# A hand-written instruction order dealt anew for the first two batches of a fused attention and SwiGLU kernel

## The chip, the cores and the metric

The kernel runs on one core of a Trainium2 chip. The metric is the device time of one execution in microseconds. TensorE (PE in the profile), VectorE (DVE), ScalarE (ACT), GpSimd (POOL) and SyncE (SP) each take their instructions in the order in which the program issued them; transfers are started from the queues of SP and ScalarE (SPq and ACTq).

## What is computed

Eight batches of 512 tokens and 32 state slots, 8 heads of 64. Tokens read the states, the states read the tokens, and the 8 x (512 + 32) rows that come out pass an RMS norm and a SwiGLU layer (512 to 1536 to 512). The reference, cut to what matters:

```python
a = softmax(scale * x @ state.T)          # per batch and head
xread = a @ state                         # 512 token rows
a2 = softmax(scale * state @ x.T)
sread = a2 @ x                            # 32 state rows
r = rows of [xread, sread], heads side by side   # (8*544, 512)
rn = r / sqrt(mean(r*r) + 1e-6) * rms_g
out = (silu(rn @ w_gate) * (rn @ w_val)) @ w_out
```

## The kernel before, in words

Everything stays in SBUF in a feature-major layout, one batch after another. Softmax reads are kept as weights over the state slots (aT_s), so the hidden layer of a batch is the product of aT_s with the batch's own weights: w_gate and w_val times the batch's states (own_weights, product at L695, ScalarE copy at L707). The three weight matrices come in 64-bit words; 18 pieces are converted to 32 bits in the first stretch, the exponent on ScalarE (exponents(), L246, L249, L252) and the mantissa on VectorE (values(), L273, L276, L282). values() also loads the next raw piece (L212) and stores the finished w_m to w_d (L286), both on SP's queue.

Batch 0 runs with plain products of 512 columns (ORDER). Batches 1 to 7 use seven products of half size in place of eight (hidden_seven), and the output layer the same twice over (project_twice), with sums of weights made at the end of ORDER and in batch 1 and fetched back from DRAM (w<-t_d, L1091). FIRST is batch 1, PERIOD batches 2 to 6, LAST batch 7, STATES the 256 state rows.

**What sets the order.** No scheduler: each part of the work is a Python generator that yields after a step, and a string of letters says which generator goes on next. One letter issues all the instructions of a step, on whatever engines it has, and its transfers. Each engine works off its own instructions in that order and waits (by semaphore) for data and for a free buffer or PSUM bank. So a letter's place in the string is its place in every queue that it uses. A number behind a letter counts that letter from the start of its string: h17 is the 17th h.

Letters of ORDER (400 steps):

| letters | work |
|---|---|
| a, b | batch 0's token read, first and second 256 tokens. a1 transposes the states' rows (L463); a4, a7, b1, b4 transpose x (L499), a5, a8 and the like copy it, a6, a9 are scores (L504); a10 maximum, a11 and b8 subtraction (L512), a12 and b9 exponential; a13 to a15 gram matrix and scaled states; then, a16 on and b10 on: sum (L522), reciprocal, scaling (a18, b12, L527), transposes (a19, b13, L532), a ScalarE copy (a20, b14, L535), gram product (a21, b15, L539), VectorE product (a22, b16, L543), sums of squares (a23, b17, L548), a24, b18 (L552), the power on GpSimd (a25, b19, L299), a26, b20 spread along rows (L306), the last scaling (a27, b21, L558) |
| s, S | batch 0's and batch 1's states read: s1 scores (L568), s2, s3 copies (L574), s4, s5 maxima (L588), s6 (L591), s7, s8 exponentials (L595; S4, S5), s9, s11 transposes (L605), s10, s12 copies (L607), s13 and s14 products over the tokens, s15 scaling (L631 and on) |
| A | batch 1's token read: A1 to A10 transposes of states and x (L317, L328) and copies (L330), A11 scores, copies (L369), A18, A21 exponentials (L411), A31 a product over the states (L437) that takes four PSUM banks |
| e, d | exponents in three steps a piece, values in four, the third of them (d3, d7, ...) without an instruction; piece 0 goes in two halves (e1 to e6, d1 to d8) |
| v | batch 0's own weights, a product and two copies for each of 6 pairs (v1, v4, v7, ...) |
| h, t, u | batch 0's hidden layer, 12 blocks: h(2m+1) gate and h(2m+2) value products (L738), t(m+1) Silu on ScalarE (L744), u(m+1) gated product on VectorE (L748). Two PSUM buffers turn in these products, so a gate product waits for the t of the block before, a value product for its u |
| p, c | output layer of batch 0 (L945), two steps a block, copies and stores (L962) |
| k, Q, w | sums of the output weights on VectorE (L988, then quarters, L1100), slot sums of batch 1 (L760) and its own weights for the first two pairs |
| z | one dummy product of the identity matrix in a bank that nothing reads (L1281); 16 of them |

Letters of FIRST (326 steps):

| letters | work |
|---|---|
| h, t, u | hidden layer in sevens: products of four 256-wide parts (L842); t copies banks to g and c (L889, L892, L894) and applies Silu (L896); u sums and gates on VectorE (L905 to L930) |
| v, x | own weights of batch 1's pairs 2 to 5: product (L695); copies and GpSimd sums (L707, L722) |
| a, s | batch 2's reads: a3 to a6 VectorE transposes (L338), a7 the write to x_d (L340) and a8 to a11 the reads back (L345), both on ScalarE's queue, a12 scores; s: the write to e_d (L616) and four reads back (L620), on ScalarE's queue too (s8 is the first) |
| p, c, k, o | output layer in seven times seven (L1146), copies (L1159), sums, stores (L1257) |
| q, G, g, f, l, w | quarters of the output weights and their fetch (L1091), fetches of w_m from w_d (L195), loads of a later batch, batch 2's first own weights |

The piece of code that reads the strings:

```python
for stream in ORDER:
    if stream in "ckw" and "s" not in seven:
        early.close()
        open_late()
    next(streams[stream])
```

Of the kernel before, what the change touches and what calls it, by code (L numbers as in the profile page):

```python
# [22 lines left out]
FLAT = 1793.0  # L23

ORDER = (
    "zzaaazazbabaeaadbdbaababbzeeeadazbedbabzszezazzbbeadadzbsdaebzzdbeabddzeabdeabAs"
    "zaAeeAadAAbabesavdAabvvAAaAhhssddstdedhueeedAdptddedddpdheuveddvvpdeheeAtedpdAed"
    "dehAedhAheutdAddeApSvdAdApuSvesAdppAvhedAddetdeAsAsehshuAedhtdedpdesdpvevAuvepsd"
    "sdedhdddedseAehApteeduddAAddhAephdveddpetvveudeAAphhAdSAedddthedpduAAAAdeedtdhvA"
    "SupdeSSvevShtAdhAhhdAkSkkkkAutAkSSupAwkkSwkskSpQpQwpQpQkcQQQwScswQpSkcQpwcwwQQQw"  # L30
)

PERIOD = (
# [4 lines left out]
)  # L38

FIRST = (  # L40
    "vahtaqhhaqataaxhthqhuavhquuqhttxhqhutxhhqtuhauuaqhuhaqahtGthqxtxuqhqftuqfhuquxhh"
    "tqtuqvauaGhahhaaaasuthxxtuhhutshxtuauhaafhuthutGvagxhhkaukksxhuhuxthuaatthhutuhh"
    "uhuuutppukuuhpuupkpkpkpfspkpakppkpapcppkkskckpppkakkppapaappckakaapckppkpkpkaspk"
    "pasgkaacckpapakgpgoagpkppksklkapppagpakkakospsopskoppapkklsswwswkpgxxxppopxoxcfc"
    "fxssoo"
)
LAST = (
    "vhhtfthhthxuhguxhtvvhutuhxfhtuthuhhuhhxtuthfxhtuxtxuhxhuhuvtauhhhthxuuthkxthuhhh"
# [1339 lines left out]
```

## Time and profile before

| | us |
|---|---|
| three runs | 744.66, 746.24, 746.92 |
| their median | 746.24 |
| the profiled execution's own time | 744.98 |
| its span in the trace | 743.0 |
| TensorE busy in it | 735.2 (99%) |
| VectorE busy | 578.5 (78%) |
| ScalarE busy | 379.7 (51%) |
| GpSimd busy | 258.9 (35%) |

The span runs from the first to the last recorded instruction, so it lies 2.0 us under the execution's time. Times in rows of a timeline are microseconds from the span's start. A row gives start, duration, engine, source line, operation, what is written and read, and how many instructions it joins; brackets hold the idle time ahead of it and what ended it. Matmuls overlap in the pipeline, so the distance from start to start says more of TensorE's pace than a duration. In the table by stretch, a row has the stretch, its length, the busy time of PE, PEld (loading of weights), DVE, ACT and POOL with the number of instructions, TensorE's granted clock, the busy share of the transfer engines, and GB/s.

### The profile page before, as it was taken

To read this page: it belongs to the slowest core of one execution; us is meant where nothing else is said; L and a number is where in the kernel's file an instruction comes from. 1 tells how busy PE (TensorE), PEld (TensorE's weight loads), DVE (VectorE), ACT (ScalarE), POOL (GpSimd) and SP (SyncE) were. 2 spreads that over 40 slices of the span, in tenths; PEclk is the share of its full clock that TensorE was granted. 3 is DMA by queue.
4 is the path that set the end of the run, shared out by engine and by line. 5 is a ranking of instruction groups with operands and counts; after the bars stand their busy time and mean duration, and the time that the engine had idled before them with its cause. 6 is when DMAs were issued, how large, how long until landed. Compare 5 with 4: busy or idle time off the path is not lost.

```text
span 743.0 us, 14235 instructions
## 1 busy us (share of the span) xinstructions
PE 735.2 (99%) x5582; PEld 590.6 (79%) x5582; DVE 578.5 (78%) x957; ACT 379.7 (51%) x635; POOL 258.9 (35%) x362
## 2 busy tenths in 40 slices
PE   8999999999999999999999999999999999999998
PEld 6634444779977998789878997799778987899996
DVE  3998989899846994699659984799469955798862
ACT  5999982473265725472366426562547336511220
POOL 3100005431373128512563228312841267324400
PEclk9999999999999999999999999999999999999999
DMA  9997936964792278607881669328860883063311
GB/s 294 279 328 239 355 158 228 322 281 134 204 343 61 91 284 278 199 1 297 234 294 28 232 207 319 93 90 299 272 188 4 315 230 130 1 223 117 133 55 28
DMA packets 60994, 146.15 MB, mean 197 GB/s; under 512 B 14848, under 2 KB 31744, under 8 KB 54016
## 3 DMA queue, kind: packets, MB, share of 16 engines
q1 hardware_dynamic: 47808, 125.78, 48.9%
q10 hardware_dynamic: 13120, 19.47, 9.4%
q8 instruction: 44, 0.72, 0.4%
q14 instruction: 22, 0.18, 0.1%
HBM read 116.46 MB, written 28.77 MB: 195 GB/s over the span
## 4 chain that ended last, share of the span: by engine, by line
PE 94%; DMA 3%; DVE 1%; ACTq 0%; issue 0%; ACT 0%; SPq 0%
PE f L842 36%; PE f L1146 31%; PE pv L738 6%; PE f L945 5%; PE pv L695 3%; PE f L1008 2%; DMA x_d<-xB 2%; PE at L695 2%; PE at L631 1%; PE f L1281 1%; PE at L355 1%; PE at L437 1%; DVE w L1100 1%; DVE xB L338 1%; DMA rows<-in_state_dram 1%; PE pv L504 1%
## 5 line engine op out<-in xcount | busy, mean ns | idle before, releaser
L842 PE MATMUL f<-aT_s,v 128*128 128x256 f32 x504 | 119.0, 381 | 0.1
L842 PEld LDWEIGHTS f<-aT_s,v 128*128 128x128 f32 x504 | 94.8, 191 | 19.6 <-DVE h L1200 4.2
L905 DVE TENSOR_TENSOR g<-g,f 128x512 f32<-128x512 f32 x84 | 55.9, 684 | 64.0 <-PE f L842 40.3
L842 PE MATMUL f<-aT_t,vs 128*128 128x256 f32 x336 | 86.7, 382 | 0.5 <-ACT g L889 0.5
L1174 POOL TENSOR_TENSOR kept<-kept 128x256 f32<-128x256 f32 x28 | 20.9, 745 | 182.8 <-DVE kept L1186 116.1
L1159 ACT COPY kept<-f 128x512 f32<-128x512 f32 (+1 forms) x56 | 30.0, 538 | 98.3 <-PE f L1146 97.6
L1146 PE MATMUL f<-w,h 128*128 128x128 f32 x588 | 74.7, 276 | 0.0
L842 PEld LDWEIGHTS f<-aT_t,vs 128*128 128x128 f32 x336 | 62.9, 190 | 13.1 <-issue 5.0
L722 POOL TENSOR_TENSOR vs<-v 128x256 f32<-128x256 f32 x42 | 31.1, 740 | 115.0 <-ACT v L707 114.8
L1146 PEld LDWEIGHTS f<-w,h 128*128 128x128 f32 x588 | 69.8, 192 | 1.2 <-issue 0.8
L896 ACT ACTIVATE hb<-g 128x1024 f32<-128x1024 f32 x42 | 44.5, 1058 | 48.1 <-DVE g L905 44.4
L918 DVE TENSOR_TENSOR hb<-hb,f 128x512 f32<-128x512 f32 (+1 forms) x48 | 31.2, 650 | 27.9 <-PE f L842 27.9
L299 POOL TENSOR_TENSOR ri<-ss,mhalf 128x4 f32<-128x4 f32 (+1 forms) x9 | 9.3, 1029 | 124.3 <-ACT ss L387 102.6
L945 PE MATMUL f<-wo,hb 128*128 128x512 f32 x96 | 44.5, 600 | 0.0
L738 PE MATMUL pv<-aT_s,v 128*128 128x512 f32 x96 | 43.9, 596 | 0.0
L842 PE MATMUL f<-aT_t,v 128*128 128x256 f32 x168 | 43.6, 382 | 0.0
L842 PE MATMUL f<-aT_s,vs 128*128 128x256 f32 x168 | 43.4, 381 | 0.0
L1146 PE MATMUL f<-wo,hb 128*128 128x128 f32 x336 | 42.3, 275 | 0.0
L1146 PE MATMUL f<-wo,h 128*128 128x128 f32 x336 | 42.1, 275 | 0.0
L1146 PEld LDWEIGHTS f<-wo,hb 128*128 128x128 f32 x336 | 40.4, 192 | 0.4
L918 DVE TENSOR_TENSOR hb<-hb,c 128x512 f32<-128x512 f32 (+1 forms) x48 | 35.7, 744 | 6.0 <-ACT hb L896 5.7
L1146 PEld LDWEIGHTS f<-wo,h 128*128 128x128 f32 x336 | 39.8, 192 | 0.0
(227 smaller groups left out, 1637.0 us busy)
## 6 DMA issues: line engine op xcount, KB each, us to landing
w_m<-w_d SPq DMA_DIRECT2D x48, 1024.0 KB
w<-t_d SPq DMA_DIRECT2D x49, 576.0 KB
out_dram<-kept SPq DMA_DIRECT2D x28, 256.0 KB
raw<-in_moe_w_val_dram SPq DMA_DIRECT2D x6, 1024.0 KB
raw<-in_moe_w_out_dram SPq DMA_DIRECT2D x6, 1024.0 KB
w_d<-w_m SPq DMA_DIRECT2D x6, 1024.0 KB
x_b<-in_x_dram SPq DMA_DIRECT2D x6, 1024.0 KB
x_d<-xB ACTq DMA_DIRECT2D x6, 1024.0 KB
```

The costliest lines, as they stand in the source:

```text
L695: TE.matmul(out=pv[e][Ns * j:Ns * j + Ns, :], lhsT=stT_g[b][D * e:D * e + D, j, :], rhs=w[D * e:D * e + D, j].rearrange("p m k f -> p (m k ...
L722: GE.tensor_tensor(out=vs[:, 0], in0=a21, in1=a22, op=ALU.add)
L738: TE.matmul(out=to[0], lhsT=lhs(i, k), rhs=r, start=(i == 0), stop=(i == len(rhs) - 1))
L842: TE.matmul(out=ps[:, i, 0:half], lhsT=l[:, i, :], rhs=r, start=(start and i == 0 and k == 0), stop=(k == len(lhs) - 1), skip_group_check= ...
L896: SE.activation(out=hb[:, 2 * mp:2 * mp + 2, 0:n].rearrange("p m (c t) -> p m c t", c=2), in_=q["g"][:, :, :, 0:half], func=ACTF.Silu if s ...
L905: VE.tensor_tensor(out=to, in0=to, in1=q[ps][:, :, 0:half], op=ALU.add)
L918: VE.tensor_tensor(out=part, in0=part, in1=val, op=ALU.mult)
L945: TE.matmul(out=banks[r], lhsT=hb[:, m, P * r:P * r + P], rhs=wo[:, m, :], start=(m == 0), stop=(m == NM - 1))
L1008: TE.matmul(out=banks[name][:, r, :], lhsT=lhs(k)[:, P * r:P * r + P], rhs=rhs(k), start=(start and r == 0 and k == 0), stop=(k == HM - 1) ...
L1146: TE.matmul(out=to[half][:, slot, :], lhsT=lhs[:, k, :], rhs=rhs[:, k, :], start=(fresh and n in (0, 4) and k == 0), stop=(k == QM - 1), s ...
L1159: SE.copy(of_half(k, i), banks[name][i])
L1174: GE.tensor_tensor(out=k[:, 4:8:3], in0=k[:, 5:6].to_broadcast([P, 2, QD]), in1=k[:, 4:8:3], op=ALU.add)
```

## The change

Only two strings are different: ORDER, which covers batch 0 and the start of batch 1 and 2 (the profile up to 126.9 us), and FIRST, batch 1 (up to 210.4 us). Each holds the same letters as often as before, each generator still runs its own steps in its own order, and PERIOD, LAST and STATES are untouched. So the program has the same instructions, and what differs is how the streams interleave in each queue.

```diff
@@ -23,11 +23,11 @@
 FLAT = 1793.0
 
 ORDER = (
-    "zzaaazazbabaeaadbdbaababbzeeeadazbedbabzszezazzbbeadadzbsdaebzzdbeabddzeabdeabAs"
-    "zaAeeAadAAbabesavdAabvvAAaAhhssddstdedhueeedAdptddedddpdheuveddvvpdeheeAtedpdAed"
-    "dehAedhAheutdAddeApSvdAdApuSvesAdppAvhedAddetdeAsAsehshuAedhtdedpdesdpvevAuvepsd"
-    "sdedhdddedseAehApteeduddAAddhAephdveddpetvveudeAAphhAdSAedddthedpduAAAAdeedtdhvA"
-    "SupdeSSvevShtAdhAhhdAkSkkkkAutAkSSupAwkkSwkskSpQpQwpQpQkcQQQwScswQpSkcQpwcwwQQQw"
+    "zzzaaazazbabaaabdebdbadeabeazszbbeadebeezdzbazzaabbaszeabbazzddbebeaaezbddabddsa"
+    "eAbzAAdaeasAbAaeAvsavvbaAdsdAdsAhdtdAhehudpdpeedthdeededdevupddvevpddAeehdeddteh"
+    "dAAAdeheuAAdeSSedhddpvAtudAdeAAvvpdphhdAshAAteshAueepdetpSedesAeddAdedpsdduddsde"
+    "psvevvdedpAhsddeedddtheeeAedehvsvuvAeAhddpddtpAduedpheAAdAedAehdAhtSddSAdevvdvuA"
+    "phhtAdheSudAheAtAtdphkkuSkAkkkkuAkSSASkwkpSwQsQwpQppwwpskSQpcQkSQScpcQQwQcwwQwQQ"
 )
 
 PERIOD = (
@@ -38,11 +38,11 @@
 )
 
 FIRST = (
-    "vahtaqhhaqataaxhthqhuavhquuqhttxhqhutxhhqtuhauuaqhuhaqahtGthqxtxuqhqftuqfhuquxhh"
-    "tqtuqvauaGhahhaaaasuthxxtuhhutshxtuauhaafhuthutGvagxhhkaukksxhuhuxthuaatthhutuhh"
-    "uhuuutppukuuhpuupkpkpkpfspkpakppkpapcppkkskckpppkakkppapaappckakaapckppkpkpkaspk"
-    "pasgkaacckpapakgpgoagpkppksklkapppagpakkakospsopskoppapkklsswwswkpgxxxppopxoxcfc"
-    "fxssoo"
+    "vaaahahatthhqxthaxuqhahutthtxuhquuqhtahqhaauqahluvtvuhhhtquxqqqhttqxuhqxquhxqufx"
+    "hhtahqtuqahhxuthaautsahahuuhtGahtvuauthkaahuxauhuhxtshhuautgxuahkhtuGthtkhuuuhuu"
+    "khutppushpuupukapkkkppkkcakpppcpkkfpkkGppagkpppppaapsaakpkpckfpapkfkckasokppaaaa"
+    "kpsscskpappapkpgpppgksskagaoppkcagppksaakppkaapwpkpspskskwoxkwxkxppxpfxokglcopsc"
+    "foxsoo"
 )
 LAST = (
     "vhhtfthhthxuhguxhtvvhutuhxfhtuthuhhuhhxtuthfxhtuxtxuhxhuhuvtauhhhthxuuthkxthuhhh"
```

The moves that the prediction speaks of:

- **Up to h1**: the third z stands ahead of a1 (two were there before). d5 goes ahead of b10; d6 and d8 go behind a18 and b16; d10 goes ahead of a22; s5 goes up 11 places, ahead of a26, and d13 down 8.
- **ORDER after h1**: t4 goes behind A15 and e30; p8 and s9 behind h11; s8 behind A21, ahead of t5; v13 ahead of s15; t8 behind e50; t10, which stood ahead of S4 and S5, behind them and e55; the k steps are mixed with u12 and others.
- **FIRST**: v3 ahead of h17; s8 up by 21 places, ahead of c6 and a43; f2 to f4 down by 40 to 120 places, behind G2 and g2; l1 up past stores; steps of h, t, u, q, x by a few places each.

## Prediction

> **What bounds the kernel now.** I read the page first, then a table of busy time by stretch, then the timelines of single engines. From the page: the span, TensorE's row, and the chain that ended last.
>
> ```profile
> span 743.0 us, 14235 instructions
> ...
> PE 735.2 (99%) x5582; PEld 590.6 (79%) x5582; DVE 578.5 (78%) x957; ACT 379.7 (51%) x635; POOL 258.9 (35%) x362
> ...
> PE 94%; DMA 3%; DVE 1%; ACTq 0%; issue 0%; ACT 0%; SPq 0%
> ```
>
> The table by stretch is cut where the kernel changes: up to the first product of the hidden layer (29.5), the rest of ORDER (126.9), then FIRST, with 2 us of it apart. After the length come the engines' busy times.
>
> ```profile
> 0.00:29.50 29.50, 25.90 (x171) 20.07 (x171) 17.95 (x37) 20.61 (x30) 7.75 (x37) 1.00 0.94 281
> 29.50:126.90 97.40, 97.40 (x481) 41.22 (x483) 86.87 (x120) 80.17 (x102) 9.35 (x9) 1.00 0.74 269
> 126.90:143.00 16.10, 16.10 (x110) 11.76 (x110) 13.07 (x23) 7.21 (x13) 6.26 (x9) 1.00 0.92 322
> 143.00:145.00 2.00, 1.53 (x8) 1.06 (x7) 1.48 (x4) 1.97 (x4) 0.00 (x0) 1.00 0.98 179
> 145.00:210.40 65.40, 65.37 (x583) 55.82 (x582) 56.17 (x99) 30.58 (x59) 25.21 (x33) 1.00 0.65 212
> ```
>
> TensorE idles 0.5 us between 29.5 and 210.4, and the change adds and removes no instruction. So a new order can win only in the 29.5 us before h1 and at that one hole; anywhere else it can only open holes. VectorE (86.87 of 97.40) and ScalarE (80.17) are close behind it in ORDER, so holes are easily opened.
>
> **The start.** Before h1 TensorE works beside dummies (z), and VectorE sets the pace. Its rows from the second half's scaling (b12) on, some left out; then the power on GpSimd (a25); then TensorE's transposes b13 and the first product h1:
>
> ```profile
> 18.18 0.69 DVE L527 TENSOR_TENSOR eS<-eS,z 128x512 f32<-128x512 f32 x1
> ...
> 21.23 0.68 DVE L282 SCALAR_TENSOR_TENSOR w_m<-raw,ex 128x512 f32<-128x512 f32 x1
> 21.85 0.69 DVE L543 TENSOR_TENSOR eS<-aT_s,pv 128x512 f32<-128x512 f32 x1
> ...
> 23.18 1.23 DVE L276 SCALAR_TENSOR_TENSOR raw<-top,raw 128x1024 f32<-128x1024 int32 x1
> ...
> 24.72 0.69 DVE L543 TENSOR_TENSOR eS<-aT_s,pv 128x512 f32<-128x512 f32 x1 [0.25 <-PE at L317]
> ...
> 27.92 1.42 DVE L558 TENSOR_TENSOR aT_s<-aT_s,pv 128x512 f32<-128x512 f32 x2
> 29.26 0.68 DVE L588 TENSOR_REDUCE m<-sS 128x1 f32<-128x512 f32 x1
> ```
>
> ```profile
> 26.89 1.15 POOL L299 TENSOR_TENSOR ri<-ss,mhalf 128x2 f32<-128x2 f32 x1 [1.56 <-DVE ss L552]
> ```
>
> ```profile
> 19.33 0.60 PE L532 MATMUL at<-ident,eS 128*128 128x128 f32 x4
> ...
> 29.49 1.96 PE L738 MATMUL pv<-aT_s,v 128*128 128x512 f32 x4
> ```
>
> VectorE's last scalings (a27, in the row at 27.92) end at 29.3, and h1 follows at 29.49. ScalarE's order up to its copy A8 is the same in both strings, so it moves nothing here. On VectorE, d5 goes ahead of b10, which ends b12 (the row at 18.18) 0.4 later, while b13 came behind dummies at 19.33, later than b12's end, and now has one dummy fewer ahead of it: nothing. d6 and d8 go behind a18 and b16, so VectorE reaches b16 at 21.4 instead of 21.85. But b16 needs b15's product, which hangs on ScalarE's unmoved copy and ends about 21.7: 0.4 to 0.5 us of VectorE are lost. d10 (1.23) goes ahead of a22, whose wait of 0.25 it fills. Then s5 (0.68) takes the place of d13 (0.69). Sum up to a27: +0.45 - 0.25 = +0.2. The branch over GpSimd says slightly more: a22 starts 0.35 late, so do a24, the power of 1.15 behind it and a27. I take +0.3; from below it is 0 (b16 not late), from above +0.6 (d6 alone, were nothing filled).
>
> **ORDER after h1.** A step of TensorE (h or p, four 512-wide products) costs 1.72 us: twelve rows from 47.61 to 52.76 are three steps, 5.15.
>
> ```profile
> 47.61 5.31 PE L738 MATMUL pv<-aT_s,v 128*128 128x512 f32 x12
> 52.76 1.88 PE L945 MATMUL f<-wo,hb 128*128 128x512 f32 x4
> ```
>
> Every gate product h(2m+1) waits for the copy t(m-1) that frees its bank, each value product for u(m-1), each output step p for its u. Prices of ScalarE between them (a conversion act and its closing one, and the exponential of the states):
>
> ```profile
> L246 ACT ACTIVATE lin<-raw,bounds 128x1024 f32<-128x1024 int16 x17 | 21.3, 1251 | 0.0
> L252 ACT ACTIVATE ex<-ex,bounds 128x1024 uint16<-128x1024 int16 x17 | 19.5, 1148 | 0.3
> ...
> L595 ACT ACTIVATE e<-sS,s 128x512 f32<-128x512 f32 x4 | 2.9, 727 | 0.0
> ```
>
> A table load (1.28, in a row below) stands before every change between the exponentials (L411, L595) and Silu (L744). The new string has as many changes, five in ORDER and three in FIRST, so loads cancel. I walked TensorE's new order against ScalarE's and VectorE's, adding these prices from p5, where both strings have the same work behind them (52.76 before, 53.1 now):
>
> - p5, v7, p6, p7, h9, h10 bring TensorE to h11 at 62.9. Now p8 and s9 no longer stand ahead of h11. It needs t5. ScalarE, counted from t4 (moved behind A15 and e30, to about 55.3) through a load, A18, e31, v8, v9, A21, s8 and the second load (1.28 + 0.6 + 1.25 + 3 x 0.6 + 0.7 + 1.28 + 0.6, so 7.5, and some 0.15 for A21's wait on VectorE), ends t5 at 62.95: +0.1.
> - v13 is now ahead of s15, which frees its bank. s15 follows d60 on VectorE, 83.75 against TensorE's 83.6: +0.15. Behind v13 on TensorE queue h16 and p13.
> - A31 needs all four banks; the last is freed by u8, which needs t8, now behind e50. It comes at 90.25 against 90.2: +0.05 to 0.1.
> - h21 needs t10. Before, t10 ran ahead of both exponentials of batch 1's states; now S4 and S5 and two loads stand ahead of it:
>
> ```profile
> 98.47 0.59 ACT L744 ACTIVATE t<-pv 128x512 f32<-128x512 f32 x1
> 99.08 1.28 ACT L595 ACT_TABLE_LOAD   x1
> ```
>
> t9 ends at 96.45; load 1.28, S4, S5, e55, two copies and the second load (0.72 + 0.72 + 1.25 + 2 x 0.5 + 1.28) put t10 at 102.7 to 103.3, and TensorE is there at 102.9: +0.4.
>
> The moved k steps run in VectorE's waits, with u12 behind; p21 covers them. Together +0.3 + 0.7 = +1.0 us by the end of ORDER. Each walked margin is good to perhaps 0.3, so these waits lie between 0 and 2.
>
> **FIRST.** The one hole is here. ScalarE issues the reads of x_d (a8 to a11) only once its write (a7) has landed, with t8 and t9 queued behind; h17 waits for t9.
>
> ```profile
> 131.89 0.40 ACTq L340 DMA_DIRECT2D x_d<-xB  x1
> ...
> 140.82 2.17 ACTq L345 DMA_DIRECT2D xG<-x_d  x4
> 143.99 0.57 ACT L889 COPY g<-f 128x512 f32<-128x512 f32 x1
> ```
>
> ```profile
> 142.35 1.03 PE L842 MATMUL f<-aT_t,vs 128*128 128x256 f32 x4
> 143.21 1.03 PE L842 MATMUL f<-aT_t,v 128*128 128x256 f32 x4
> 144.70 1.10 PE L842 MATMUL f<-aT_t,vs 128*128 128x256 f32 x4 [0.47 <-ACT g L889]
> ```
>
> Four products take 0.86 (142.35 to 143.21), so h17 could have started at 144.07: 0.63 lost, of which the page calls 0.47 idle. I take 0.7 with what the next steps wait. The new string sets v3 (0.9) ahead of h17, and TensorE comes 1.0 later, so it reaches h17 at about 145.9, when even a write landing 1 us later has let t9 through: -0.7. Of other moves, s8 goes up 21 places, so that ScalarE waits for e_d with c6 and a43 queued behind. The write left at 190.26 and was answered by 195.76:
>
> ```profile
> 190.26 0.35 ACTq L616 DMA_DIRECT2D e_d<-eB  x1
> ...
> 195.76 0.31 ACTq L620 DMA_DIRECT2D e<-e_d  x1
> ...
> 204.16 1.09 PE L695 MATMUL pv<-w_m,stT_g 64*32 64x512 f32 x16
> ```
>
> c6 then runs about 197; by my walk TensorE's next step into its bank (p40) comes 1.5 later: nothing, or 0.5 if that write lands 2 us later. On SP's queue f2 to f4 fall by 40 to 120 places, behind G2 and g2. g2 waits for a buffer that an outer product of the output frees, but f2 stands ahead of it, and its weights are wanted only at 204.16: nothing. l1, a small load, goes up 221 places on SP past such fetches and costs two issues there.
>
> Sum: +0.3 + 0.7 - 0.7 = **+0.3 us**. The profiled execution took 744.98 us, its span 743.0. So its like would take 745.3. The three runs before lie from 744.66 to 746.92, and 746.24, their median, is 1.26 above the profiled one. On that scale the forecast is 746.24 + 0.3, **746.5 us**: no change.
>
> **Rivals.** *The clock comes up earlier.* TensorE's first rows:
>
> ```profile
> 1.76 2.07 PE L1281 MATMUL f<-ident 128*128 128x256 f32 x4 [1.76 <-POOL ident masks.py:199]
> 5.67 0.45 PE L463 MATMUL at<-ident,rows 128*128 128x128 f32 x1 [1.83 <-DMA rows<-in_state_dram]
> ...
> 6.76 1.06 PE L499 MATMUL at<-ident,x_b 128*128 128x128 f32 x4
> 7.62 1.06 PE L1281 MATMUL f<-ident 128*128 128x256 f32 x2
> ...
> 10.47 0.61 PE L499 MATMUL at<-ident,x_b 128*128 128x128 f32 x4
> 10.92 1.00 PE L504 MATMUL pv<-apart,xT 128*128 128x64 f32 x8
> ```
>
> Four transposes take 0.86 us from 6.76 (to 7.62) and 0.45 from 10.47: TensorE runs at half speed until about 10, though the clock column reads 1.00. Full speed came some 4.2 us after the steady work that begins at 5.67. The work of 1.76 did not count, or the wait for rows undid it. The new string puts z3 into that wait and leaves 1.0 of its 1.83. If a wait so short no longer undoes it, the switch comes 4.2 after 1.76, at 6. The 4.3 us up to 10 then shrink to half, bar what was full already: -1.8 through a8, VectorE and h1, to 744.7. For it: two thirds instead of two fifths of the time from 3.1 to 6.5 are busy. Against: no row shows a switch across any wait. [...]
>
> *ScalarE becomes the bound of ORDER (slower).* Four of the margins above are under 0.2 and hang on ScalarE alone. If it comes one conversion act (1.25) later than walked at t5, h11 starts 1.25 late, and with 0.8 more at t10 the end is +2.0 over the forecast, 748.5. It decides from the point where t5 ends after 63.2. For it: ScalarE is busy 80.17 of 97.40. Against: no step of TensorE waited for it there (97.40 busy of 97.40).
>
> *The order changes nothing that TensorE feels.* Every step covered: +0 - 0.7, 745.5, inside the forecast's range.
>
> **Chances.** Forecast with its neighbours 0.44, clock 0.28, ScalarE 0.24, all covered 0.04. A measurement of this kernel tells about 0.3% (2.2 us) from no change: under 744.0 is faster, over 748.5 slower. From the forecast come 0.34 same, 0.04 faster (none of its waits of 1.0, and a little of the clock) and 0.06 slower (its waits at their upper end of 2, with one more like them). From the clock, half faster, half same, as 744.7 lies 0.7 from the bound and the waits of ORDER decide: 0.14 and 0.14. From ScalarE, with 748.5 as its smallest price, 0.18 slower and 0.06 same. All covered is same. Faster 0.18, same 0.58, slower 0.24. The range for 8 in 10 goes from 743.4 (the clock, without the waits of 0.3 and 1.0 of the forecast) to 749.0 (ScalarE, and the 0.5 of e_d); the forecast alone, 745.3 to 747.6.
>
> **What would show it.** Right: h1 0 to 0.6 later, holes before h21 and h11 under 0.5, none before h17. The clock shows in the transposes at 6.8 taking 0.45 for four. Wrong: a hole over 1 us in ORDER, a wait on a w<-t_d or w_m<-w_d transfer, h1 later than 30.3.

## The result and the profile after

The changed kernel takes 744.64 us (median of 22 runs, 742.42 to 746.50), the kernel before 746.04 (22 runs beside them, 744.06 to 747.82). The ratio is 0.9981 with an interval of 0.9974 to 0.9989: 1.4 us less, clear of zero, and less than the 0.3% that was set as the bound of "no change". The forecast was 746.5, so 0.3 more. The time lies in the range, on the other side of zero.

The profiled execution of the changed kernel took 744.53 us, that of before 744.98. So the two profiles differ by only 0.45 of the 1.4. From the page of the changed kernel: the span, the engines, the chain that ended last.

```profile
span 742.6 us, 14225 instructions
...
PE 735.6 (99%) x5582; PEld 591.0 (80%) x5582; DVE 579.0 (78%) x957; ACT 380.2 (51%) x635; POOL 260.3 (35%) x362
...
PE 98%; ACT 1%; DMA 1%; DVE 0%; SPq 0%; issue 0%; DVEq 0%
```

The transfers have nearly gone out of the chain (3% before, 1% now). The table by stretch, with the same cuts as before (columns as there; FIRST in one piece):

```profile
0.00:29.50 29.50, 26.18 (x169) 19.92 (x170) 17.91 (x36) 20.46 (x29) 8.18 (x37) 1.00 0.91 276
29.50:126.90 97.40, 97.40 (x476) 41.50 (x474) 86.06 (x118) 79.94 (x103) 8.91 (x9) 1.00 0.73 265
126.90:210.40 83.50, 83.45 (x699) 69.01 (x698) 73.40 (x127) 40.02 (x74) 30.84 (x39) 1.00 0.69 238
```

TensorE is busy for 97.40 of 97.40 us in ORDER and for 83.45 of 83.50 in FIRST. Its rows at the start, at h1, and at h17 (the row at 145.49, which has no wait in brackets now):

```profile
5.64 0.45 PE L463 MATMUL at<-ident,rows 128*128 128x128 f32 x1 [0.94 <-DMA rows<-in_state_dram]
...
6.74 1.06 PE L499 MATMUL at<-ident,x_b 128*128 128x128 f32 x4
7.59 1.06 PE L1281 MATMUL f<-ident 128*128 128x256 f32 x2
...
10.30 0.61 PE L499 MATMUL at<-ident,x_b 128*128 128x128 f32 x4
10.74 1.00 PE L504 MATMUL pv<-apart,xT 128*128 128x64 f32 x8
...
29.79 1.52 PE L738 MATMUL pv<-aT_s,v 128*128 128x512 f32 x3
```

```profile
145.49 1.03 PE L842 MATMUL f<-aT_t,vs 128*128 128x256 f32 x4
```

The four transposes from 6.74 still take 0.85 us, so full speed did not come at 6 us in this execution, as the clock rival had it. h1 starts 0.30 later, as forecast.

Where the two profiles differ, by the starts of the same products: h1 is 0.30 later (29.49, 29.79); the first product of batch 1 is 0.56 later (128.90, 129.46), so ORDER behind h1 costs 0.26; the first product of batch 2 is 0.16 earlier (210.20, 210.04), so FIRST gives back 0.72; a stall of some 0.4 at 548 in batch 6 of before, far from the change, makes the rest but for small drifts. By the profiles alone the end of batch 1 misses the forecast by 0.46 (+0.3 forecast, -0.16 measured). What the forecast did not foresee lies between the profile of before and its median, 1.06 us.

### The profile page after: what moved, and what is told of

The parts are those of the page before. It is cut to its first block, busy times and chain, and to the rows that moved or that the text cites. A ratio compares the mean times of both kernels' runs of the same rounds, so it can differ in the third digit from the quotient of the medians.

```text
span 742.6 us, 14225 instructions
## 1 busy us (share of the span) xinstructions
PE 735.6 (99%) x5582; PEld 591.0 (80%) x5582; DVE 579.0 (78%) x957; ACT 380.2 (51%) x635; POOL 260.3 (35%) x362
## 4 chain that ended last, share of the span: by engine, by line
PE 98%; ACT 1%; DMA 1%; DVE 0%; SPq 0%; issue 0%; DVEq 0%
PE f L842 40%; PE f L1146 31%; PE f L945 6%; PE pv L738 6%; PE pv L695 3%; PE at L695 3%; PE f L1008 2%; PE at L631 1%; PE at L355 1%; PE at L437 1%; DMA rows<-in_state_dram 1%; PE f L1281 0%; PE pv L504 0%; PE at L306 0%; PE at L499 0%; PE at L649 0%
## 5 line engine op out<-in xcount | busy, mean ns | idle before, releaser
L299 POOL TENSOR_TENSOR ri<-ss,mhalf 128x4 f32<-128x4 f32 (+1 forms) x9 | 9.4, 1045 | 126.9 <-issue 82.0
```

## Experiments

Two theories were set against each other. **Transfers**: before's median lies above its profile because most of its executions wait longer for the answer of the write to x_d, and the new FIRST takes this wait away; the write to e_d came into this theory only after v3_early had shown a wait there. **Clock**: the dummy that now stands ahead of a1 brings full speed earlier in part of the executions. Each run below is set beside runs of the kernel before on the same chip; medians are of 6 to 12 runs, the kernel before's of 21 to 35. "N below" is by the medians, the interval by the ratio.

### One string alone

**order_only**: ORDER new, FIRST old. 

> The new ORDER with the old FIRST. In the two profiles at hand the new ORDER alone costs 0.56 us up to the start of batch 1 (128.90 to 129.46). Theory of the transfer (before's median lies above its profile because the write to x_d lands later in most executions, so that the hole before h17 is larger than the 0.6 us of the profile): the hole stays, 0.6 us smaller by the later start, so the time is that of before within 0.3 us. Theory of the clock (the dummy ahead of the first transpose brings full speed earlier in part of the executions): the whole gain is here, 0.7 to 1.8 us below before, and the profile may show the four transposes near 6.8 us at 0.45.


Measured: 745.97 beside 745.69, ratio 0.9998 (0.9987 to 1.0008). The new ORDER alone makes no change that can be told from zero.

**first_only**: ORDER old, FIRST new. 

> The old ORDER with the new FIRST. Theory of the transfer: the whole gain is here and more, 1.4 to 2.0 us below before, since the waits of the new ORDER (0.26) and its later h1 (0.3) are not paid. Theory of the clock: only the 0.7 us of the hole seen in the profile, and the median within 0.7 of before.


Measured: 743.95 beside 745.69, ratio 0.9978 (0.9969 to 0.9987): 1.74 below. The gain is in FIRST, and by the medians it is more than twice the hole of the first profile (the interval is 1.0 to 2.3).

### The kernel before, looked at again

**before_look**: no edit. 

> The kernel before once more, for a second profile of it: three kernels with its FIRST and other edits lost 0.4 to 4.0 us in waits on the transfers over x_d and e_d, its own first profile 0.5. If those waits are what sets its median above its first profile: waits of 0.8 to 2 us in FIRST, ahead of h17 or at L306 or L631, and full speed at another moment than 10.0. If the first profile is typical: one wait of about 0.5.


Measured: one run, 746.22, which is 1.24 more than the first profiled one. TensorE's waits in FIRST are now two; rows of TensorE, and of ScalarE's queue at the write to e_d (L616) and the first read back (L620):

```profile
144.27 1.10 PE L842 MATMUL f<-aT_t,vs 128*128 128x256 f32 x4 [0.55 <-ACT g L889]
```

```profile
199.69 0.65 PE L306 MATMUL at<-ident,ri 128*128 128x128 f32 x4 [0.82 <-POOL ri L299]
```

```profile
189.84 0.36 ACTq L616 DMA_DIRECT2D e_d<-eB  x1
...
196.73 0.31 ACTq L620 DMA_DIRECT2D e<-e_d  x1
```

The write to e_d is answered after 6.9 us here; in the first profile it was 5.5. a43 stands behind that read on ScalarE, the power on GpSimd behind a43, the transposes at L306 behind the power. With 5.5 this chain ends just in time, with 6.9 TensorE stands for 0.8. The first profile showed no such wait. A third wait, of 0.79, lies at 550 in batch 6; with the stall of 0.4 that the first profile has there, it came in nine of the twenty profiles of this study, of 0.3 to 1.6 us, with either string. So the 1.24 is 1.0 of FIRST, 0.7 more in batch 6 and small drifts, less 0.5 for an h1 that came at 28.96.

How often FIRST is held longer than in the first profile is not shown. From the first product of batch 1 to that of batch 2 it took 81.30 us there, 82.31 in before_look, 81.38 and 81.37 in two versions with the same FIRST (order_only, z_early) and 86.09 in a third (z_fill). In the five profiles with the whole new FIRST it took 80.36 to 80.76.

### Which of FIRST's letters

**v3_early**: 

> The kernel before with one edit: v3, the product of batch 1's fourth pair of own weights, stands ahead of h17 rather than 26 letters behind. Theory of the transfer: as it puts 0.9 us of TensorE's work into the wait for t9, 0.6 to 0.9 us below before, and up to 0.9 in executions whose write lands late; no hole at h17 in the profile. Theory of the clock: 0.5 below at most.


```diff
-"...uhaqahtGthqxtxuqhqftuqfhuquxhhtqtuqvaua..."
+"...uhaqahtGtvhqxtxuqhqftuqfhuquxhhtqtuqaua..."
```
Measured: 745.24 beside 745.69, ratio 0.9992 (0.9984 to 1.0001), less than the 0.6 to 0.9 expected and not clear of zero. Its profiled run was its slowest (746.53): a hole of 1.4 at h17 in spite of v3, since ScalarE took 3.9 us there to issue the four reads of x_d, and 0.8 at L306.

**xd_clear**: 

> The kernel before with one edit in FIRST: the third to eighth q step and the first G go later, so that no store of weight quarters (t_d) and no fetch of one starts beside the write to x_d; before, a t_d store of 576 KB leaves 0.1 us behind that write and the fetch ahead of its landing. v3 stays behind h17. If what runs beside the write makes it slow: the write lands 7 to 8 us after its issue in place of 8.9, the hole ahead of h17 is under 0.3 us, and the time is 0.5 to 0.9 below before. If the write's time is its own: 8.5 to 9 us still, hole and time as before.


```diff
-"vahtaqhhaqataaxhthqhuavhquuqhttxhqhutxhhqtuhauuaqhuhaqahtGthqxtxuqhqftu..."
+"vahtaqhhaqataaxhthhuavhuuhttxhhuqqtxhhtuhaquuahuhaqahttqqhqqxtxuqhqfGtu..."
```
Measured: 747.54 beside 746.01, ratio 1.0018 (1.0007 to 1.0028), 1.5 slower. The write to x_d was answered in 7.4 us in place of 8.9, as the first answer expected, and no wait is left at h17. But three other waits stand in this profile (0.5 on hb, 0.9 on c, 0.7 at L631). What the edit takes away from beside the write is a fetch, issued 2 us ahead of the answer, and a store of 576 KB; in the kernel before the store leaves 0.1 us behind the write:

```profile
132.00 0.32 SPq L1102 DMA_DIRECT2D t_d<-w  x1
```

In the twelve profiles that have the store 0.1 to 0.6 us behind the write, and the fetch before its answer, the answer took 8.5 to 11.2 us; in the eight that have neither, 7.0 to 8.1. So the slow write goes with these two, and no run parts them. The edit as a gain is not shown.

**store_early**: 

> The kernel before with one edit in FIRST: the first output store of 256 KB stands ahead of the fourth g rather than behind, so it leaves near 184 and not 0.1 us ahead of the write to e_d. If the transfers beside that write make it late and GpSimd's power and the transposes at L306 with it: the write is answered in 4 to 5 us rather than 5.5 to 6.9, no wait on the power at L306, and 0.3 to 0.8 below before. If that wait is chance of another kind: the time of before within 0.2.


```diff
-"...papakgpgoagp..."
+"...papakgpogagp..."
```
Measured: 745.73 beside 746.01, ratio 0.9990 (0.9981 to 1.0000). The write to e_d was answered after 6.8 us without the store, with 0.36 of wait at L306. So it is not the store by itself.

**ed_later**: 

> The kernel before with one edit in FIRST: the write to e_d goes behind two copies of ScalarE (c5, c6), so it leaves near 191.7 rather than 190.3, some 2 us and not 0.5 behind the fetch of 576 KB (g) that SP issues near 189.7. In five profiles with that fetch 0.5 us ahead the write was answered after 5.5 to 6.9 us, in four with it 2.1 us ahead after 3.1 to 4.3. If the fetch beside it makes the write slow: answered in 3 to 4.5 us, near 195.5 for all its later start, no wait at L306, and 0.3 to 0.8 below before. If the write has its own time: answered at 197 or later, waits of 0.8 us and more at L306, and 0.3 to 1 above before.


```diff
-"...kaspkpasgkaacckpapak..."
+"...kaspkpagkaaccskpapak..."
```
Measured: 745.12 beside 745.79, ratio 0.9999 (0.9990 to 1.0008): no change by the ratio, though the medians lie 0.67 apart. The write left 1.4 us behind the fetch (191.49), and was answered at 196.86, after 5.4. That is 1.1 later than in the first profile of before and 0.1 later than in the second, for leaving 1.2 and 1.65 later; it was not answered sooner.

**v3_ed**: 

> The edit of ed_later and that of v3_early together (v3 ahead of h17): two letters of FIRST out of 326. If the two transfer waits are all that the new FIRST takes away: 1.0 to 1.7 below before, near the new FIRST alone (1.74 below). If it needs more (the q steps later, the stores): 0.3 to 0.9 below.


Measured: 745.38 beside 745.79, ratio 0.9994 (0.9985 to 1.0003). The write was answered after 6.1, with a wait of 0.8 at L306 and none at h17. The two letters alone are not the gain.

**l1_early**: 

> The kernel before with one edit in FIRST: l1, the load of a later batch's state rows (two transfers of 32 KB in short packets), goes from its place at 194.8 us, while the write to e_d is under way, to 157 us; the new FIRST has it at 136. If these loads hold up the write's end: the write answered in 3 to 4.5 us in place of 5.4 to 6.9, near 194.5, no wait at L306, and 0.3 to 0.8 below before. If not: answered in 5.4 to 6.9 us, a wait of 0.4 to 0.8 at L306 in most executions, and the time of before within 0.2.


```diff
-"...fhuthutGvagxhhk..."   and   "...pkppksklkapp..."
+"...fhuthutGlvagxhh..."   and   "...pkppkskkapp..."
```
Measured: 745.99 beside 745.94, ratio 0.9997 (0.9988 to 1.0006). The write was answered after 5.4. So it is not the loads of rows by themselves.

**v3_l1_store**: the edits of v3_early, l1_early and store_early. 

> Three edits of FIRST together: v3 ahead of h17, l1 at 157 us, and the first output store ahead of the fourth g. If the loads of rows (with or without the store) make the second wait and v3 covers the first: no wait at L306, one of at most 0.5 at h17, and 1.0 to 1.7 below before, near the new FIRST alone. If the write to e_d has another cause: a wait at L306 in the profile still, and 0.3 to 0.9 below, from v3 and the store.


Measured: 745.14 beside 745.94, ratio 0.9993 (0.9984 to 1.0002). The write was answered after 5.9, with no wait at L306 and 0.6 at h17. These are the waits of the first answer, but the time is 0.8 below by the medians, short of its 1.0 to 1.7, and not clear of zero.

**v3_back**: ORDER old, FIRST new but for v3. 

> The old ORDER and the new FIRST with one edit: v3 directly behind h17 instead of two products ahead of it, so that TensorE reaches h17 some 1 us earlier. If v3 as cover for t9's wait carries the new FIRST's gain: a hole of 0.5 to 1.3 us at h17 and 0.5 to 1.0 above the new FIRST alone (743.95), so 1.0 below before. If the transfers' own course (the write to x_d answered in 7.4 us in place of 8.9) carries it: no hole or one under 0.3, and within 0.4 of the new FIRST alone.


```diff
-"...ahluvtvuhhhtquxqqqhttqxuh..."
+"...ahluvtuhhhtquxqqqhvttqxuh..."
```
Measured: 744.63 beside 745.66, ratio 0.9988 (0.9978 to 0.9998): 1.0 below before, so 0.7 short of first_only by the medians. There is no hole at h17, and 0.43 at L306; the write to x_d was answered in 7.0. That fits neither answer in full: the shorter write left no hole for v3 to cover here, and yet the time is above first_only. The two intervals overlap, so a share of v3 in the gain is not shown.

### The two halves of FIRST

**new_head**: 160 letters of the new FIRST, the rest in the old one's order. 

> FIRST in two halves: the first 160 letters of the new string, then what is left in the order of the old one. The first half holds the hidden layer's products, the write to x_d and its reads; of the second half's order only what the first 160 left out is moved. If the gain of the new FIRST (1.74) lies at the write to x_d: 1.2 to 1.8 below before, no wait at h17. If it lies half at x_d and half at e_d: 0.7 to 1.1 below, and a wait of 0.4 to 0.8 at L306 in most executions.


Measured: 744.46 beside 745.90, ratio 0.9979 (0.9970 to 0.9989), 1.4 below. ScalarE's queue at the two writes and their first reads, then TensorE's waits in batch 1:

```profile
131.90 0.37 ACTq L340 DMA_DIRECT2D x_d<-xB  x1
139.46 2.62 ACTq L345 DMA_DIRECT2D xG<-x_d  x4
...
189.48 0.35 ACTq L616 DMA_DIRECT2D e_d<-eB  x1
196.27 0.31 ACTq L620 DMA_DIRECT2D e<-e_d  x1
```

```profile
198.87 0.65 PE L306 MATMUL at<-ident,ri 128*128 128x128 f32 x4 [0.45 <-POOL ri L299]
203.77 1.10 PE L631 MATMUL at<-x_b,e 128*32 128x64 f32 x64 [0.90 <-DMA e<-e_d]
```

**new_tail**: the other way round. 

> FIRST in two halves: the first 160 letters of the old string, then what is left in the order of the new one. If the gain lies at the write to x_d: within 0.4 of before, waits of 0.5 to 1.4 at h17, and no wait at L306. If it lies half at each: 0.6 to 1.0 below, the write to e_d answered in 3.1 to 4.3 us.


Measured: 745.17 beside 745.90, ratio 0.9988 (0.9979 to 0.9997), 0.7 below. The same rows:

```profile
132.38 0.40 ACTq L340 DMA_DIRECT2D x_d<-xB  x1
142.23 2.11 ACTq L345 DMA_DIRECT2D xG<-x_d  x4
...
193.20 0.35 ACTq L616 DMA_DIRECT2D e_d<-eB  x1
196.19 1.28 ACTq L620 DMA_DIRECT2D e<-e_d  x3
```

```profile
146.06 1.10 PE L842 MATMUL f<-aT_t,vs 128*128 128x256 f32 x4 [1.34 <-ACT g L889]
```

The answer times part cleanly between the halves. The new head answers x_d in 7.6 us and leaves e_d at 6.8, with waits at L306 and L631. The new tail answers e_d in 3.0 and leaves x_d at 9.8, with a wait of 1.34 at h17. By the medians the head is worth twice the tail, but the intervals overlap, and each of these two profiled executions was slower than its median, with a FIRST of 81.95 and 82.10 us. In the whole new FIRST both answers are short (7.4 and 3.8 us in the changed kernel); from first_only:

```profile
131.71 0.38 ACTq L340 DMA_DIRECT2D x_d<-xB  x1
139.13 2.45 ACTq L345 DMA_DIRECT2D xG<-x_d  x4
...
190.78 0.35 ACTq L616 DMA_DIRECT2D e_d<-eB  x1
194.35 1.28 ACTq L620 DMA_DIRECT2D e<-e_d  x3
```

Over all twenty profiles: with the old head x_d took 8.5 to 9.8 us (11.2 in z_fill, below; 7.4 in xd_clear), with the new head 7.0 to 8.1. With the old tail e_d took 5.3 to 6.9, with the new one 3.0 to 4.3.

### The clock and the start

**z_early**: 

> The kernel before with one edit: the ninth dummy, one of those ahead of the transposes at 19.3 us, stands ahead of the first transpose a1. Theory of the clock: 0.7 to 1.8 us below before. Theory of the transfer: no change, within 0.2 us, and the full speed near 10 us as before.


```diff
-"zzaaazazbabaeaadbdbaababbzeeeadazbedbabzszezazz..."
+"zzzaaazazbabaeaadbdbaababbzeeeadazbedbabzszeazz..."
```
Measured: 745.00 beside 745.69, ratio 0.9988 (0.9977 to 0.9998). Full speed came at about 8.9 in its profile, but at 8.7 to 9 too in v3_early and v3_back, which have two dummies there, and at 9.6 to 10.7 in order_only, first_z and the changed kernel, which have three.

**first_z**: that edit and the new FIRST. 

> The old ORDER with its ninth dummy ahead of a1, and the new FIRST: the two edits that were faster alone. If both gains stand and are of different places: 2.0 to 2.8 below before, so 742.9 to 743.7, and below the changed kernel by about 1. If the gain of the early dummy was the chance of its runs: as the new FIRST alone, 1.4 to 2.0 below.


Measured: 743.86 beside 746.01, ratio 0.9975 (0.9959 to 0.9992), with first_only at 743.95 beside 745.69. That is 2.15 below by the medians, where 2.0 to 2.8 was expected if both gains stand and 1.4 to 2.0 if not; the early dummy adds nothing that can be told.

**z_fill**: three dummies more than before. 

> The kernel before with three dummies more, five instead of two ahead of the first transpose, so that TensorE is busy without a hole from 1.77 on and a1 starts some 0.4 us late. [...] If the dummies do not count: full speed near 9 to 10.7 as in the other five profiles and 0.1 to 0.4 above before.


```diff
-"zzaaazaz..."
+"zzzzzaaazaz..."
```
Measured: 746.33 beside 746.01, ratio 1.0003 (0.9990 to 1.0016): no gain. TensorE at the start:

```profile
1.77 4.60 PE L1281 MATMUL f<-ident 128*128 128x256 f32 x10 [1.77 <-POOL ident masks.py:199]
6.20 0.28 PE L463 MATMUL at<-ident,rows 128*128 128x128 f32 x1
6.32 0.60 PE L1281 MATMUL f<-ident 128*128 128x256 f32 x2
6.75 0.60 PE L499 MATMUL at<-ident,x_b 128*128 128x128 f32 x4
7.19 0.60 PE L1281 MATMUL f<-ident 128*128 128x256 f32 x2
```

Four transposes from 6.75 take 0.44 us: full speed from about 6.2, 4.4 us after steady work began. h1 came at 27.98, 1.5 earlier. And in FIRST it was all lost: FIRST took 86.09 us in this execution, 4.8 more than in the first profile (the execution took 748.63, 2.3 above the version's median):

```profile
145.13 1.10 PE L842 MATMUL f<-aT_t,vs 128*128 128x256 f32 x4 [2.38 <-ACT g L889]
```

```profile
206.42 1.10 PE L631 MATMUL at<-x_b,e 128*32 128x64 f32 x64 [1.21 <-DMA out_dram<-kept]
```

```profile
130.40 0.40 ACTq L340 DMA_DIRECT2D x_d<-xB  x1
141.61 1.80 ACTq L345 DMA_DIRECT2D xG<-x_d  x4
```

The write left 1.5 us earlier than before and was answered 0.8 later. In the eleven other profiles with the old head (xd_clear not counted) it left between 131.2 and 133.1, and the answers came from 140.3 to 142.2. In this execution the earlier start only waited there.

**first_fill**: the same dummies and the new FIRST. 

> The new FIRST, and the old ORDER with three dummies more ahead of the first transpose. With the old FIRST these dummies brought h1 to 27.98 and lost it all in FIRST (waits of 4.0 us, the x_d write answered at 141.6). If the new FIRST has room for an earlier start: h1 near 28.0, waits in FIRST under 1 us, and 2.5 to 3.2 below before (742.8 to 743.5). If the transfers bound batch 1 whatever its order: waits of 1 us and more, and within 0.4 of the new FIRST alone.


Measured: 742.92 beside 745.66, ratio 0.9962 (0.9947 to 0.9977), 2.7 below. h1 came at 28.44, and FIRST has no hole:

```profile
126.90:210.40 83.50, 83.50 (x695) 69.77 (x673) 71.38 (x123) 40.45 (x75) 32.65 (x42) 1.00 0.70 236
```

This version is faster than the kernel before. Beside the changed kernel it was not run: against the kernel before the two ratios are 0.9962 (up to 0.9977) and 0.9981 (from 0.9974), so a lead over the changed kernel is likely and not shown.

**after_fill**: the changed kernel with two dummies more. 

> The changed kernel with two dummies more ahead of the first transpose (five, without a hole up to a1). [...]


Measured: 743.15 beside 745.66, ratio 0.9965 (0.9954 to 0.9975), 2.5 below, which is not told apart from first_fill. h1 at 29.09, so 0.7 before the changed kernel's.

## Why the prediction was wrong

**The sum by its own profile: near, and in part by luck.** The start was forecast at +0.3, and h1 came 0.30 later. But in the thirteen profiles with the old ORDER as it was, h1 lay between 28.85 and 29.96, earlier where full speed came earlier (at 8.7 in v3_back, at 11.0 in new_tail), and with the new ORDER it came at 29.79 and 30.25 (order_only). That this one pair of profiles agrees to the hundredth is luck. The hole at h17 was put at -0.7, and FIRST became 0.72 shorter from profile to profile, without a hole before h17. The four waits of ORDER were put at +0.7 together; ORDER behind h1 became 0.26 longer. h11, v13 and A31 show no wait by the starts of their products. h21 starts 0.05 behind the end of t10 and costs some 0.2 where 0.4 was forecast, and the products of v7 at 54.8 take 0.14 longer, which the forecast did not have. The signs that the prediction named for being right (h1 0 to 0.6 later, no hole over 0.5 before h11 or h21, none before h17) all came, and the median still moved the other way. The narrower range for the forecast alone (745.3 to 747.6) does not follow from its terms either: waits of 0 to 2 less 0.7 give 745.5 to 747.5.

**The step that failed: from the profile to the median.** The prediction said of the median that it "is 1.26 above the profiled one. On that scale the forecast is 746.24 + 0.3". That takes the distance for scatter that any order would have, and carries the term of FIRST over as the one profile shows it. By the medians FIRST is worth some 1.0 us more than that (0.3 to 1.6 by the interval), so most of the distance is time in FIRST that the one profile did not hold and that the new order removes; among the five profiles with the old FIRST as it was, before_look and z_fill show it. On the median the terms are: ORDER, start included, +1.0 forecast, +0.28 measured in order_only (0.9987 to 1.0008, so from -1.0 to +0.6 us); FIRST, -0.7 forecast, -1.74 measured in first_only (-2.3 to -1.0). Their sum, -1.46, is near the -1.4 measured for both. So the term of FIRST was less than half of what it measured, and that of ORDER too large by 0.4 us at least.

**The term that was missed: e_d.** The prediction put the moves about s8 at "nothing, or 0.5 if that write lands 2 us later". The row that spoke was quoted there: a write answered after 5.5 us, with the chain behind it ending just before TensorE came. It was read as a cost that the move might add. In the kernel before it was a wait that already stood in other executions: in before_look, and in six of the thirteen profiles with the old tail, most of them with another edit (0.4 to 0.8 at L306; 0.7 to 1.2 at L631 in three). With the new tail, and an answer in 3.0 to 4.3 us, little of it is left: 0.25 and 0.43 at L306 in two of seven profiles.

**x_d: the cover named is not what removed the hole.** v3 was named as cover, and the margin was worked out for "even a write landing 1 us later". But v3_back, without that cover, has no hole at h17, its write being answered in 7.0 us; with the cover and a write of 9.2 us there was a hole of 1.4 in v3_early, of 0.6 in v3_l1_store and none in v3_ed. That the write itself would be answered 1.5 us sooner, as one of q's stores to t_d and a fetch no longer run beside it, was not seen: the q steps and G were passed over as moves without a price. new_head (1.4 below) against new_tail (0.7) puts the greater part of FIRST's gain there by the medians, with intervals that overlap; what v3 adds to it is not shown (v3_early 0.45, not clear of zero).

**The rivals.** The clock: its condition was that a wait of about 1 us no longer undoes the dummies' work. The changed kernel, order_only and first_z, with such a wait, came to full speed at 9.6 to 10.7 and speak against it, and z_early at 8.9 came no earlier than v3_back, which waits 1.75; z_fill, with no wait, came to it at 6.2. Nor is the moment fixed by the string: the same two dummies gave 8.7 in one execution (v3_back) and 10.7 in another (xd_clear). That z_early measured 0.7 lower stays open, as first_z did not repeat it. ScalarE as the bound of ORDER: no wait of more than 0.2 in ORDER. The clock's 744.7 is the number nearest to the measured 744.64, and that is chance: the profile of the changed kernel shows full speed at 9.6, not at 6. All covered (745.5) is nearest in its terms, with no waits in ORDER and the gain in FIRST; it was given the least chance, 0.04.

**What stays open.** What in the new tail takes the wait for e_d away. The store, the rows' loads, and a lead of 1.4 us over the fetch ahead of it are each ruled out as the sole reason. In every profile the answer came 5.1 to 7.5 us after the issue of that fetch, whether the write left 0.5 to 0.6 us behind it (old tail), 1.4 (ed_later, v3_ed) or 2.1 (new tail): 5.1 to 6.4 with the new tail, 5.9 to 7.5 with the old. So much of the shorter time is the write's later start, and not an earlier answer; in the changed kernel it came 5.9 us after the fetch, in the first profile of before 6.0. The landing marks in the traces say the same: the last mark of the write came 1.2 to 1.4 us behind the last one of the fetch in sixteen of the twenty profiles, whenever it left (0.6 to 1.9 in the others): at 195.69 behind 194.34 in the first profile of before, at 195.35 behind 194.09 in the changed kernel. What ties the two marks together, no run shows.

## What to carry to other kernels

Before a forecast is put on the scale of the median, ask what makes one execution differ from the next: where a profiled run lies below the median, look for waits on transfers that it just missed, and count the margin of every chain behind a DRAM round trip as a wait that other executions may have. A letter that starts a transfer can have a price in the answer time of a write beside it: 1.5 us here, for the write to x_d (8.9 in before, 7.4 in xd_clear and in the changed kernel). Count an answer time from what stands ahead of the write as well as from its own start. And an earlier start may be worth nothing until the next place that is held by a transfer has room for it (h1 came at 27.98 in z_fill, which measured 0.3 above before by the medians, and at 28.44 in first_fill, which measured 2.7 below).

## What the runs showed of the hardware

- TensorE's full speed came 6.2 to 7.5 us into the span when it worked without a hole from 1.77 on, and 8.7 to 11.1 when it waited 0.8 to 1.9 us for the first rows, in a different place in each execution. The clock column reads 1.00 through all of it (up to 126.9 us in before, z_fill and first_fill).
- One and the same write of 1 MB to x_d was answered in 8.5 to 11.2 us with a store of 576 KB issued 0.1 to 0.6 us behind it and a fetch before its answer, and in 7.0 to 8.1 without them.
- One and the same write of 512 KB to e_d was answered in 5.3 to 6.9 us when it left 0.5 to 1.4 us behind a fetch of 576 KB, and in 3.0 to 4.3 when it left 2.1 behind; from the fetch's issue it was 5.1 to 7.5.
